# One core, two chained models: GpSimd's first load delayed, batch 0's softmaxes in parts, another order, and 40 pairs of unread matmuls

## The chip, the cores and the metric

The kernel runs on one core of one Trainium2 chip. The metric is device time in microseconds (us) of one execution; lower is better. Three runs of the kernel before gave 136.5 to 136.55, median 136.54. A separate execution was profiled; its own time was 136.75.

The core's engines work through queues of their own and wait for each other by semaphores: TensorE (PE; its weight loads are listed as PEld), VectorE (DVE), ScalarE (ACT), GpSimd (POOL) and SyncE (SP). SP, GpSimd and ScalarE can start transfers, which 16 DMA engines carry out.

## The reference

```
p_packed = softmax(scale * p @ k^T) @ v              # per batch and head: 32 rows attend to 576
x        = softmax(scale * q @ p_packed^T) @ p_packed   # 576 rows attend to the 32
x        = heads side by side: (8, 576, 512)
W        = scale * (x @ w_q) @ (x @ w_k)^T           # 576 x 576 per batch
out      = relu(W @ x) @ w_out                       # (8, 576, 512), float32
```

There are 8 batches, 8 heads, 576 positions, 64 numbers a head. All inputs and the output are float32; the kernel computes in bfloat16 behind its loads, with float32 sums.

## The kernel before, in words

One batch is one pass through about 70 small operations. Nothing is looped over them: the string SCHEDULE (lines 10 to 55) holds all operations of all 8 batches in one order, written `name@batch`, with the PSUM banks behind a colon (`s0` and `e0` use one buffer of three banks, psA, in turns) and the engine of an eviction as a last letter (v: VectorE, s: ScalarE). Lines 641 to 651 issue them in that order. Each engine takes its own from the string in order, so an instruction that waits holds up everything behind it on its engine.

The operations of a batch, in the order in which its data goes through them:

- LK, LV, LQ (L138): loads of K, V and Q with a cast to bfloat16, from GpSimd's queue, 576 KB each as landed, into six buffers per tensor. cw and wo load the weights in the same queue.
- kt, qt (L261): transposes of K and Q on TensorE, three parts each; ke, qe evict them from PSUM.
- s0 (L283): p times K. nm0 (L297): row maximum on VectorE. ex0, ex1 (L300): exponential on ScalarE, one per head half. rc1: reciprocal of the sums.
- xt, xe, pv, pp, pt, pte (L314 to L370): transposes of the exponentials, product with V, scaling, transposes of the packed rows; pq, pqe: their product with the mixer's weights.
- e0 (L388): Q times the packed rows. mx0, sb0, sm0, rr0 (L409 to L429): maximum, subtraction, sum and reciprocal on VectorE, x0 the exponential on ScalarE, ml0 to ml2 (L431) the division on GpSimd in three parts.
- at, ae, wk, wke, wkx, wq, wqe, g, ge, y, ye (L448 to L556): the mixer on the packed rows.
- m0, m1, m2 and r (L558 to L595): the mixed rows and their relu; o0 to o4 and oe (L597 to L611): the product with w_out and its eviction; st, sc (L613 to L632): stores from SP's queue, in blocks of 256 or 128 KB. m2, o4 and st2 exist once for two batches.

Batch 0 has a start of its own. SP loads p of batch 0 (p_f, L153), K of batch 0 in float32 in two halves (k_f, L156) and the whole of p (p_c, L161). cA and cB cast k_f (L216), kf and kfe transpose and evict it (L221, L231). tp and lp (L182, L188) put p of batch 0, transposed, into pT_bd, which holds p of all batches as the weights of s0; pc, tr and lq (L194 to L213) do that for the other seven. VectorE sets pT_bd and the two masks to zero and one (L164 to L172), while GpSimd makes the identity matrix (L177) behind its first load.

Of the kernel before, what the change touches and what calls it, by code (L numbers as in the profile page):

```python
# [9 lines left out]
SCHEDULE = """  # L10
    LK@1 cw2@0 LV@0 tp@0:0 LQ@0 lp@0v LK@2 cw0@0 cA0@0s cA1@0v LV@1 kf1@0:0 kf0@0:1 kfe1@0s
    LQ@1 kfe0@0v cB1@0s cB0@0s kf3@0:1 kfe3@0s kf2@0:0 kfe2@0s pc1@0v pc0@0v s0@0 LV@2 tr@0:01
    nm0@0 cw3@0 kt0@1:2 lq0@0s kt2@1:3 ke0@1v kt1@1:4 ke2@1v ex1@0 lq1@0v cw1@0 ex0@0 ke1@1v
    rc1@0 xt0@0:4 s0@1 xe0@0v xt1@0:1 nm0@1 xe1@0s qt0@0:4 LK@3 qt1@0:3 qt2@0:1 qe0@0v ex0@1
    pv@0:02 qe1@0v qe2@0s pp0@0 ex1@1 pp1@0 kt1@2:0 LK@4 rc1@1 pt@0:2 ke1@2v xt1@1:1 pte@0s
    kt0@2:3 wo0@0 xe1@1s xt0@1:4 ke0@2v kt2@2:2 e0@0 xe0@1v ke2@2v mx0@0 pv@1:24 LQ@2 sb0@0
    pp0@1 x0@0 s0@2 pp1@1 qt0@1:2 nm0@2 wo1@0 pt@1:4 qt2@1:3 pte@1s qt1@1:1 qe2@1s qe0@1v ex1@2
    sm0@0 ex0@2 LV@3 qe1@1v xt0@2:2 rc1@2 xt1@2:3 rr0@0 LV@5 pq@1:1 xe0@2v pq@0:4 xe1@2s e0@1
    LK@5 pqe@0s pqe@1s pv@2:32 mx0@1 ml2@0 ml0@0 pp1@2 kt2@3:1 ml1@0 pp0@2 at0@0:2 ke2@3s sb0@1
    kt0@3:4 pt@2:3 kt1@3:0 LQ@3 ae0@0s at1@0:1 pte@2s ke1@3v x0@1 pq@2:3 ae1@0v ke0@3v kt2@4:0  # L20
    LQ@4 pqe@2s wk@0:1 sm0@1 ke2@4s s0@3 wke@0s wq@0:0 LV@4 wkx@0 kt0@4:3 rr0@1 wqe@0s kt1@4:1
# [12 lines left out]
    ml1@3 kt0@7:3 pte@4s qe1@5v kt1@7:4 pq@4:2 ke0@7v qt0@6:1 ml2@3 pqe@4s qt2@6:0 ml0@3 ke1@7v
    at1@3:2 qe2@6s qe0@6v e0@4 ae1@3v g@2:1 mx0@4 at0@3:2 ge@2s qt1@6:0 ae0@3s y@2:1 pv@5:43
    ye@2v qe1@6v m0@2:12 sb0@4 wq@3:0 r00@2s r01@2s wk@3:1 pp0@5 wqe@3s s0@7 wkx@3 wke@3s pp1@5
    x0@4 o1@2:0 nm0@7 kt0@6:3 oe1@2s kt2@6:1 pt@5:4 ke0@6v ex0@7 kt1@6:0 sm0@4 o0@2:2 pte@5s
    ex1@7 qt0@7:4 pq@5:3 ke1@6v pqe@5s e0@5 qe0@7v ke2@6s oe0@2v g@3:3 m1@2:40 ge@3s mx0@5
    xt1@7:2 st0@2 r11@2s y@3:3 xt0@7:1 r10@2s qt2@7:0 xe0@7v xe1@7s o2@2:4 rr0@4 qe2@7s ye@3v
    ml0@4 o3@2:2 rc1@7 sb0@5 oe2@2s m2@3:4 ml1@4 oe3@2s at0@4:0 qt1@7:3 ae0@4v x0@5 s0@6 st1@2  # L40
    qe1@7v ml2@4 m0@3:02 nm0@6 pv@7:31 r2@3s r00@3s o4@3:4 r01@3s sm0@5 ex1@6 o1@3:2 oe4@3s
    pp0@7 pp1@7 at1@4:0 ex0@6 st2@3 o0@3:4 rr0@5 ae1@4v oe1@3s ml2@5 rc1@6 pt@7:1 ml1@5 oe0@3v
    wq@4:0 pte@7s wk@4:2 wqe@4s st0@3 ml0@5 pq@7:4 wkx@4 wke@4s xt0@6:1 pqe@7s at1@5:0 xe0@6v
    xt1@6:2 at0@5:4 ae1@5v xe1@6s e0@7 ae0@5s g@4:2 mx0@7 m1@3:01 ge@4s pv@6:43 r11@3s r10@3s
    sb0@7 y@4:1 wq@5:2 o3@3:0 wqe@5s pp0@6 x0@7 o2@3:2 pp1@6 ye@4v pt@6:3 oe3@3s sm0@7 wk@5:1
    pte@6s m1@4:04 oe2@3s pq@6:3 e0@6 wke@5s wkx@5 st1@3 r10@4s rr0@7 g@5:1 r11@4s mx0@6
    m0@4:02 ml0@7 ge@5s pqe@6s o3@4:4 r01@4s ml2@7 r00@4v ml1@7 y@5:2 o2@4:3 oe3@4s sb0@6
    o0@4:4 oe2@4s ye@5v x0@6 at1@7:3 st1@4 oe0@4v m2@5:2 o1@4:0 ae1@7v r2@5s sm0@6 at0@7:3
    oe1@4s o4@5:2 ae0@7s st0@4 m0@5:04 rr0@6 oe4@5s m1@5:31 r00@5v ml2@6 r01@5s wk@7:2 st2@5
    ml1@6 r11@5v r10@5s wq@7:4 wke@7s wkx@7 o1@5:1 ml0@6 wqe@7s at1@6:4 oe1@5s o0@5:2 ae1@6v  # L50
    at0@6:4 oe0@5v o3@5:1 ae0@6s st0@5 wk@6:4 oe3@5s g@7:2 wkx@6 wke@6s o2@5:1 ge@7s y@7:2
    wq@6:4 oe2@5s ye@7v g@6:3 wqe@6s st1@5 m1@7:12 ge@6s m0@7:40 r10@7s r11@7v y@6:3 r01@7s
    ye@6v o3@7:2 r00@7v o2@7:0 o1@7:4 oe2a@7v oe2b@7s m2@7:3 o0@7:1 oe1@7s sc2@7 r2@7s m0@6:40
    oe3@7s oe0@7v o4@7:3 sc1@7 r01@6s r00@6v m1@6:01 oe4a@7v oe4b@7s sc3@7 o0@6:4 r11@6s r10@6s
    o1@6:1 sc0@7 oe0@6v o3@6:0 oe1@6s st2@7 o2@6:1 oe3@6s st0@6 oe2@6s st1@6
"""

SLOTS = dict(
    k_sb=6, v_sb=6, q_sb=6, kT=3, qT=3, e1T=2, e1=2, pp=4, ppT=4, pqk=4, e2=2, a2=3, a2T=2,
    wk=2, wkx=3, wqT=2, g=2, y=3, reluT0=2, reluT1=2, reluX=2, o_sb0=2, o_sb1=2, ox=2,  # L60
    nmax=4, rsum=4, rrec=4, mx=2, rs=2, rr=2
# [4 lines left out]
def kernel(  # L66
# [12 lines left out]
    nc = tc.nc  # L79
# [12 lines left out]
    L = p.shape[2]  # L92
# [26 lines left out]
    def tile(name, shape, dtype, b, key=None):  # L119
        key = key or name  # L120
        if key not in S_[b]:
            S_[b][key] = sbp.tile(shape, dtype, tag=f"{name}{(b // 2 if name in PAIRED else b) % SLOTS[name]}", name=name)
        return S_[b][key]
# [36 lines left out]
    p_c = sbp.tile([P, 16, Dh], fp32, name="p_c")  # L160
    nc.sync.dma_start(p_c, p.rearrange("b h (lh lo) d -> (b h lh) lo d", lo=16))  # L161

    pT_bd = sbp.tile([P, B, 4, 2, L], bf16, name="pT_bd")
    nc.vector.memset(pT_bd, 0.0)  # L164
# [5 lines left out]
    nc.vector.memset(hmask, 0.0)  # L170
    for h2 in range(2):
        nc.vector.memset(hmask[64 * h2:64 * h2 + 64, :, h2], 1.0)  # L172

    ident_f = sbp.tile([P, P], fp32, name="ident_f")
    ident = sbp.tile([P, P], bf16, name="ident")

    def make_ident():  # L177
        make_identity(nc, ident_f)
        nc.vector.tensor_copy(ident, ident_f)
# [14 lines left out]
    for i in range(2):  # L194
        ops[f"pc{i}"] = lambda b, on, i=i: evict(on, p_b[:, 8 * i:8 * i + 8], p_c[:, 8 * i:8 * i + 8], scale=scale)
# [100 lines left out]
    @op  # L296
    def nm0(b):  # L297
        nc.vector.tensor_reduce(tile("nmax", [P, 2], fp32, b), S_[b]["s1"], axis=AX, op=MAX, negate=True)  # L298
# [109 lines left out]
    @op  # L408
    def mx0(b):  # L409
        nc.vector.tensor_reduce(tile("mx", [P, NU, 1], fp32, b), S_[b]["e"], axis=AX, op=MAX)  # L410

    @op
    def sb0(b):
        nc.vector.tensor_tensor(  # L414
            tile("e2", [P, NU, L], fp32, b), S_[b]["e"], S_[b]["mx"].to_broadcast((P, NU, L)), op=SUB
        )

    @op
    def x0(b):
# [262 lines left out]
```

## Time and profile before

| | |
|---|---|
| median of three runs | 136.54 us |
| the profiled execution: its time, its span | 136.75 us, 135.0 us |
| TensorE busy | 106.2 us (79%) |
| VectorE busy | 97.3 us (72%) |
| ScalarE busy | 88.2 us (65%) |
| GpSimd busy | 41.0 us (30%) |
| DMA written | 25.73 MB, 191 GB/s over the span |
| granted TensorE clock, mean | 0.97 |

The span runs from the first instruction to the last; the profiled execution's time has 1.75 us around it. A profile line such as "L288 PE MATMUL s<-kT,pT_bd" names the line of the kernel, the engine, the operation, and the tile written and the tiles read; evictions all carry the lines of one helper (L128 to L136) and are told apart by their tiles. In a timeline each row has the start, the busy time, the engine, the line, the operation and its count, and in brackets how long the engine had been idle and what released it. The rows of stages give a stretch, its length, the busy time of PE, PEld, DVE, ACT and POOL with their counts, the granted TensorE clock, the share of the DMA engines and GB/s.

### The profile page before, as it was taken

How to read it: one execution, taken by the hardware profiler on the slowest of the kernel's cores; microseconds unless marked ns; L12 is line 12 of the kernel's file. 1: busy time of each engine (PE TensorE's matmuls, PEld its weight loads, DVE VectorE, ACT ScalarE, POOL GpSimd, SP SyncE). 2: the span in 40 equal slices, each digit the busy share in tenths (PEclk: the TensorE clock that was granted, in tenths of full speed). 3: DMA queues.
4: the chain of work that ended last, by engine and by line, in shares of the span. 5: the costliest groups of instructions: out<-in, count | busy, mean ns of one | idle time of the engine just before them, and what ended most of it. 6: DMA issues, size and time to landing. Idle time of an engine off the chain costs nothing.

```text
span 135.0 us, 4579 instructions
## 1 busy us (share of the span) xinstructions
PE 106.2 (79%) x1993; PEld 77.1 (57%) x1993; DVE 97.3 (72%) x167; ACT 88.2 (65%) x175; POOL 41.0 (30%) x59
## 2 busy tenths in 40 slices
PE   1228668954988999999679985999999999999900
PEld 0216657843767568778458653675866656563400
DVE  5413767999899949999769985999699994445200
ACT  3244808247687996986765693999789895818610
POOL 6924124226938522154033000153302442000000
PEclk9999968999999999999999999999999999999985
DMA  3999999999999999999999998554702386655994
GB/s 50 306 311 208 207 205 207 208 199 212 202 211 198 207 209 246 313 210 247 278 206 252 236 208 150 113 130 124 195 5 61 112 215 162 174 144 114 205 222 164
DMA packets 18277, 25.73 MB, mean 191 GB/s; under 512 B 2512, under 2 KB 14800, under 8 KB 18256
## 3 DMA queue, kind: packets, MB, share of 16 engines
q0 software_dynamic: 13776, 14.22, 63.0%
q1 hardware_dynamic: 4480, 11.21, 29.9%
q8 instruction: 15, 0.25, 0.7%
q14 instruction: 6, 0.05, 0.1%
HBM read 30.21 MB, written 9.44 MB: 294 GB/s over the span
## 4 chain that ended last, share of the span: by engine, by line
PE 42%; DMA 31%; DVE 11%; ACT 6%; issue 3%; SPq 1%; DVEq 0%; ACTq 0%
DMA q_sb<-in_q_dram 22%; PE o_ps L602 13%; PE tp_h L266 6%; DMA k_f<-in_k_dram 5%; DMA out_dram<-o_sb 4%; PE tp_x L319 3%; PE s L288 3%; ACT o_sb L130 2%; PE pv L339 2%; DVE kT L136 2%; DVE e L414 2%; PE wq_ps L514 2%; PE e_ps L401 2%; DVE pp L347 2%; PE wk_ps L492 1%
## 5 line engine op out<-in xcount | busy, mean ns | idle before, releaser
L433 POOL TENSOR_TENSOR a<-e,rr 128x512 bf16<-128x512 f32 (+1 forms) x24 | 19.3, 832 | 41.7 <-DVE rr L429 37.7
L602 PE MATMUL o_ps<-w_out,reluT 128*64 128x512 bf16 x256 | 31.3, 380 | 0.3 <-DVE reluT L132 0.2
L602 PEld LDWEIGHTS <-reluT 128*64 128x64 bf16 x256 | 14.9, 110 | 10.6 <-issue 1.0
L130 ACT ACTIVATE o_sb<-o_ps 128x512 f32<-128x512 f32 (+1 forms) x24 | 14.0, 596 | 6.7 <-PE o_ps L602 3.8
L130 ACT ACTIVATE reluT<-m_ps 128x512 bf16<-128x512 f32 x25 | 13.8, 603 | 1.6 <-PE m_ps L564 1.6
L266 PE MATMUL tp_h<-ident,q_sb 128*64 128x128 bf16 x288 | 11.4, 229 | 2.5 <-DMA q_sb<-in_q_dram 2.5
L302 ACT ACTIVATE e1T<-s,nmax 128x576 bf16<-128x576 f32 x16 | 12.1, 755 | 0.8 <-DVE nmax L298 0.7
L266 PE MATMUL tp_h<-ident,k_sb 128*64 128x128 bf16 x252 | 10.4, 222 | 2.6 <-ACT wk L130 1.2
L266 PEld LDWEIGHTS <-q_sb 128*64 128x64 bf16 x288 | 9.9, 117 | 4.4 <-DMA q_sb<-in_q_dram 3.6
L298 DVE TENSOR_REDUCE nmax<-s 128x2 f32<-128x1152 f32 x8 | 10.8, 1347 | 1.9 <-PE s L288 1.9
L136 DVE COPY kT<-tp_h 128x768 bf16<-128x768 bf16 (+1 forms) x18 | 9.6, 548 | 3.3 <-PE tp_h L266 2.0
L421 ACT ACTIVATE e<-e 128x1152 f32<-128x1152 f32 x8 | 9.3, 1161 | 4.1 <-DVE e L414 4.1
L410 DVE TENSOR_REDUCE mx<-e_ps 128x36 f32<-128x1152 f32 x8 | 10.8, 1348 | 1.6 <-PE e_ps L401 1.5
L266 PEld LDWEIGHTS <-k_sb 128*64 128x64 bf16 x252 | 8.8, 110 | 4.0 <-DMA k_sb<-in_k_dram 2.2
L414 DVE TENSOR_TENSOR e<-e_ps,mx 128x1152 f32<-128x1152 f32 x8 | 10.8, 1350 | 0.2
L425 DVE TENSOR_REDUCE rs<-e 128x36 f32<-128x1152 f32 x8 | 10.8, 1344 | 0.2 <-ACT e L421 0.2
L319 PE MATMUL tp_x<-ident,e1T 128*64 128x128 bf16 x144 | 6.9, 232 | 4.4 <-DVE kT L136 2.3
L136 DVE COPY qT<-tp_h 128x768 bf16<-128x768 bf16 x16 | 8.4, 546 | 2.6 <-PE tp_h L266 2.6
L140 POOL DMA_DIRECT2D v_sb<-in_v_dram x8 | 6.0, 752 | 13.6 <-DMA v_sb<-in_v_dram 4.6
L136 DVE COPY o_sb<-o_ps 128x512 f32<-128x512 f32 (+1 forms) x9 | 6.0, 661 | 5.7 <-PE o_ps L602 3.8
L339 PE MATMUL pv<-v_sb,e 64*128 64x256 bf16 x144 | 9.2, 270 | 0.5 <-DVE kT L136 0.3
L288 PE MATMUL s<-kT,pT_bd 128*64 128x64 bf16 (+3 forms) x64 | 7.0, 328 | 1.9 <-DVE e L414 1.5
(86 smaller groups left out, 209.5 us busy)
## 6 DMA issues: line engine op xcount, KB each, us to landing
out_dram<-o_sb SPq DMA_DIRECT2D x28, 256.0 KB, 3.6
v_sb<-in_v_dram POOLq DMA_DIRECT2D x8, 576.0 KB, 18.0
q_sb<-in_q_dram POOLq DMA_DIRECT2D x8, 576.0 KB, 20.8
k_sb<-in_k_dram POOLq DMA_DIRECT2D x7, 576.0 KB, 16.0
k_f<-in_k_dram SPq DMA_DIRECT2D x2, 576.0 KB, 5.6
out_dram<-ox SPq DMA_DIRECT2D x8, 128.0 KB, 2.7
out_dram<-o_sb SPq DMA_DIRECT2D x8, 128.0 KB, 2.4
p_c<-in_p_dram SPq DMA_DIRECT2D x1, 512.0 KB, 8.8
```

What stands on the lines that cost most here:

```text
L130: nc.scalar.activation(dst, src, func, scale=scale)
L136: nc.vector.tensor_copy(dst, src)
L266: nc.tensor.transpose(tp[64 * g2:64 * g2 + 64, 2 * gp:2 * gp + 2, jj, :], S_[b][src][:, gp + 2 * g2, order[3 * t + jj]], ident,)
L288: nc.tensor.matmul(ps[64 * gp:64 * gp + 64, S * h2 + c0:S * h2 + c1], pT_bd[:, b, 2 * gp + h2].rearrange("d g l -> d (g l)"), S_[b]["kT"][ ...
L298: nc.vector.tensor_reduce(tile("nmax", [P, 2], fp32, b), S_[b]["s1"], axis=AX, op=MAX, negate=True)
L302: nc.scalar.activation(tile("e1T", [P, 2, S], bf16, b)[:, h2], S_[b]["s1"][:, h2], EXP, bias=S_[b]["nmax"][:, h2:h2 + 1], accum_out=rsum[: ...
L319: nc.tensor.transpose(tp[64 * h2:64 * h2 + 64, j - j0, :], S_[b]["e1T"][:, h2, 64 * j:64 * j + 64], ident,)
L339: nc.tensor.matmul(ps[h2], S_[b]["e1"][r, j, :], S_[b]["v_sb"][r, :, j, :].rearrange("s (g gp) d -> s gp g d", gp=2), start=(j == 0), stop ...
L410: nc.vector.tensor_reduce(tile("mx", [P, NU, 1], fp32, b), S_[b]["e"], axis=AX, op=MAX)
L414: nc.vector.tensor_tensor(tile("e2", [P, NU, L], fp32, b), S_[b]["e"], S_[b]["mx"].to_broadcast((P, NU, L)), op=SUB)
L433: nc.gpsimd.tensor_tensor(tile("a2", [P, NU, L], bf16, b)[:, r], S_[b]["e2"][:, r], S_[b]["rr"][:, r].to_broadcast((P, r.stop - r.start, L ...
L602: nc.tensor.matmul(ps[64 * g2:64 * g2 + 64], src[:, i, o + 64 * g2:o + 64 * g2 + 64], w_out[:, i, :], start=(i == 0), stop=(i == 3),)
```

## The change

What it does:

- GpSimd makes the identity matrix first, then sets pT_bd to zero and fills hmask (VectorE did both), and only then issues its first load, which is Q of batch 0 and no longer K of batch 1.
- p_c has no buffer of its own any more: it takes that of the second half of k_f, and is loaded when the last cast of k_f (cB1) is done.
- For batch 0, nm, mx, sb, x, sm and rr are split into two instructions each (A and B: head halves, or units 0 to 15 and 16 to 35).
- wm issues pairs of 512-column matmuls (identity times the first 512 columns of pT_bd) whose result nothing reads: 13, 3, 2, 5, 4, 2, 6, 1 and 4 pairs at nine places of the first part of the list.
- The whole list has another order, with other banks and other engines for some evictions. Stores of a block (sc) may be issued from ScalarE's queue; two of the last block's four are.

The diff, cut to its core:

```diff
+    LQ@0 tp@0:4 wm@13:0 LV@0 cw3@0 cw1@0 cA0@0s cA1@0v LK@1 lp@0v LK@2 kf0@0:4 wm@3:0 cw2@0
+    cB0@0s cB1@0v LQ@1 kfe0@0v kf3@0:3 kf1@0:2 kfe3@0s kf2@0:4 kfe1@0v wm@2:0 kfe2@0v pc1@0s
+    s0@0 pc0@0s wm@5:0 nmA@0 nmB@0 ex0@0 qt0@0:1 cw0@0 ex1@0 qt2@0:3 qe0@0v qt1@0:4 qe1@0s
+    rc1@0 xt1@0:0 qe2@0v xt0@0:2 xe1@0v tr@0:31 xe0@0s pv@0:40 lq0@0v lq1@0s LV@1 LK@3
+    wm@4:2 pp1@0 pp0@0 wo1@0 pt@0:2 wm@2:0 pte@0v e0@0 kt2@1:0 wo0@0 mxB@0 kt1@1:3 kt0@1:2
+    mxA@0 ke1@1s wm@6:1 sbB@0 ke2@1s sbA@0 xB@0 kt2@2:3 ke0@1v LQ@2 xA@0 kt1@2:1 smB@0 s0@1
+    ke1@2s LV@2 wm@1:0 rrB@0 ke2@2s nm0@1 kt0@2:1 ml2@0g wm@4:0 ke0@2s ml1@0g smA@0 ex1@1
+    qt0@1:1 LK@4 at1@0:4 rrA@0 ex0@1 qe0@1v pq@0:0 qt2@1:2 LV@3 qt1@1:1 qe2@1v pqe@0s
+    xt0@1:3 ml0@0g qe1@1s ae1@0v xt1@1:0 s0@2 rc1@1 xe0@1v xe1@1s at0@0:2 nm0@2 ae0@0s
+    pv@1:41 ex1@2 wk@0:0 pp1@1 pp0@1 wq@0:3 wke@0s wkx@0 ex0@2 pt@1:4 g@0:1 pte@1s ge@0v
...
+    oe1@6v st2@3 m1@7:32 o0@6:1 r10@7s r11@7v oe2@6s m0@7:03 o3@7:2 r00@7v r01@7s oe0@6v
+    o3@6:3 oe3@7s st0@6 m2@7:4 o1@7:1 r2@7s sc3@7p oe3@6s o4@7:0 oe1@7s o0@7:3 st1@6 sc1@7s
+    oe4a@7v oe4b@7v o2@7:4 oe0@7v st2@7 oe2a@7v oe2b@7s sc0@7p sc2@7s
...
-    p_c = sbp.tile([P, 16, Dh], fp32, name="p_c")
-    nc.sync.dma_start(p_c, p.rearrange("b h (lh lo) d -> (b h lh) lo d", lo=16))
+    def load_rest_of_p():
+        p_c = sbp.tile([P, 16, Dh], fp32, tag=f"q_sb{SLOTS['q_sb'] - 2}", name="p_c")
+        nc.sync.dma_start(p_c, p.rearrange("b h (lh lo) d -> (b h lh) lo d", lo=16))
+        return p_c
...
+    make_identity(nc, ident_f)
...
-    nc.vector.memset(pT_bd, 0.0)
+    nc.gpsimd.memset(pT_bd, 0.0)
...
+    for part, r in (("0", slice(0, 2)), ("A", slice(0, 1)), ("B", slice(1, 2))):
+        ops["nm" + part] = lambda b, r=r: nm(r, b)
...
+    UNITS = {"0": slice(0, NU), "A": slice(0, 16), "B": slice(16, NU)}
...
+    def wm(n, ks):
+        ps = bank(ks[0], [P, 512], fp32, "warm")
+        for _ in range(n):
+            for g2 in range(2):
+                nc.tensor.matmul(
+                    ps[64 * g2:64 * g2 + 64], ident[:, 64 * g2:64 * g2 + 64],
+                    pT_bd.rearrange("d b x g l -> d (b x g l)")[:, 0:512], start=True, stop=True,
+                )
...
+        if name == LAST_KCAST:
+            S_[0]["p_c"] = load_rest_of_p()
```

GpSimd's queue in the new order, from its first load: LQ@0 LV@0 cw3 cw1 LK@1 LK@2 cw2 LQ@1 cw0 LV@1 LK@3 wo1 wo0 LQ@2 LV@2, ml2@0 ml1@0, LK@4 LV@3, ml0@0, ml0@1 ml1@1 ml2@1, LQ@3 LK@5 LQ@4 LV@4 LK@6 LQ@6 LK@7 LQ@5, ml of batch 2, LV@5 LQ@7 LV@6, ml of batches 3 and 4, LV@7, and the other ml.

## The prediction

> **What bounds the kernel now.** I read the page's 40 slices first, then the stage table, the chain of work that ended last, and the timelines of the first 45 us and of the end.
>
> ```profile
> PE   1228668954988999999679985999999999999900
> DVE  5413767999899949999769985999699994445200
> PEclk9999968999999999999999999999999999999985
> DMA  3999999999999999999999998554702386655994
> ```
>
> Three stretches (3.4 us a slice): TensorE is thin until about 40 us, mostly full to 128 us, then idle. DMA is full to 84 us. The stage table gives sizes (the columns are PE, PEld, DVE, ACT, POOL busy):
>
> ```profile
> 0.00:10.00 10.00, 1.97 (x27) 1.44 (x27) 3.99 (x14) 3.62 (x5) 6.57 (x14) 1.00 0.84 222
> 10.00:20.00 10.00, 7.29 (x120) 5.96 (x118) 5.78 (x13) 4.29 (x11) 2.73 (x4) 0.90 1.25 207
> 20.00:30.00 10.00, 7.66 (x190) 6.78 (x187) 8.74 (x15) 4.82 (x9) 2.73 (x4) 0.93 1.26 205
> 30.00:40.00 10.00, 7.24 (x197) 6.03 (x192) 9.54 (x15) 7.61 (x17) 6.89 (x9) 1.00 1.22 207
> ...
> 128.20:135.00 6.80, 0.00 (x0) 0.00 (x0) 0.00 (x0) 0.58 (x1) 0.00 (x0) 0.68 0.71 192
> ```
>
> Of the span's 135.0 us TensorE is idle 28.8: 8.0, 2.7, 2.3 and 2.8 in these first stages, 6.2 between 40 and 128.2, and 6.8 behind its last matmul. The chain shows what ends the waits:
>
> ```profile
> 1.74 7.23 DMA k_f<-in_k_dram
> ...
> 53.67 29.52 DMA q_sb<-in_q_dram
> ...
> 83.23 0.53 PE tp_h L266 x12
> ...
> 128.18 0.60 ACT o_sb L130
> ```
>
> First the load of batch 0's K, at 83.2 us the last load of Q, and then TensorE to the end.
>
> **A yardstick.** One nominal price for each operation of the list, from uninterrupted pieces of that chain: kt, qt 0.35 us, s 0.61, xt 0.26, pv 0.99, pt 0.18, pq 0.11, e 0.63, at 0.22 and 0.34, wk and wq 0.46, g 0.30, y 0.11, m 0.33, m2 0.24, o 0.87. Both lists come to 95.1 us of TensorE without the unread pairs. "Lag" is clock time minus the nominal work ahead of a point. Before, it is 16.2 at e0@0 (9.0 us of work done at 25.2), 20.3 at e0@1 (13.2 at 33.5), 22.9 at m0@0 (22.7 at 45.6), 29.4 at qt0@7 (53.8 at 83.2), 30.3 at pv@6 (67.5 at 97.8) and 33.1 at the end (95.1 at 128.2). The last 27.6 us of work added 2.85: 0.103 per us, with TensorE full, so this is what the prices leave out.
>
> **Change 1: GpSimd starts later, K of batch 0 comes alone, p_c after it.** GpSimd now makes the identity and zeroes pT_bd and hmask ahead of its first load. No row shows a GpSimd memset of 2048 bf16. Its rows of 128x128 (225 ns) and 128x1 (102 ns) give 0.97 ns an element: 2.1 us, or 1.1 if it goes by words as DVE's row does (1024 words, 0.91 us). I take 2.1, since the change's instruction is over 2048 elements, so pT_bd is zero at 3.75 us and the first load is issued at 4.5 (before: 1.25). That row of DVE is 0.89 ns a word; "VectorE: DVE Perf Modes" (Zero memsets can be issued as uint32) of the Trainium skill says a memset costs a cycle per element whatever its type. It speaks against moving this one to an engine with no word form; by words the forecast would be 1.0 us lower. Transfers do not run dry, since k_f (1.18 MB at the 310 GB/s of slices 2 and 3) takes from about 2.7 to 6.5 us. It landed at 8.99 before, so 2.5 us seem to be won.
>
> **Change 2: 13 unread pairs come first.** They eat that. They need pT_bd, so they start at 3.75. At half clock a pair costs 0.427 us (s0@1 below: 1152 columns in 0.96 us of chain), at full clock 0.215 (o: four pairs in 0.87). All 13 slow are 5.5 us, eight slow and five fast 4.5; I take 5.25, to 9.0. lp writes pT_bd, which the pairs read, so it waits on DVE until 9.0, and cB1 is behind it: lp 0.7 to 9.7, cB1 0.55 to 10.25, kfe0 0.5, kfe1 and kfe2 0.5 each behind kf1 and kf2: s0@0 ends at 12.6 instead of 13.0.
>
> p_c is issued only behind cB1, at 10.3. Its one row:
>
> ```profile
> p_c<-in_p_dram SPq DMA_DIRECT2D x1, 512.0 KB, 8.8
> ```
>
> Before, it queued behind k_f and landed 2.1 us after it (8.99 to 11.07). A small load (p_f, 1.9 us) plus 2.1 is 4.0; the row itself is 8.8. I take 4.9, nearer the first because k_f no longer precedes it: landing at 15.2. Here is a new wait: pc1 and pc0 are now on ScalarE **ahead of ex0@0**. Queued behind them are both exponentials, and TensorE's xt@0 behind those. Two casts (0.6 each) and two exponentials (1.56 for both): 17.95, where before
>
> ```profile
> 15.06 0.74 ACT L302 ACTIVATE e1T<-s,nmax 128x576 bf16<-128x576 f32 x1
> 18.03 0.75 PE L319 MATMUL tp_x<-ident,e1T 128*64 128x128 bf16 x10 [2.33 <-DVE kT L136]
> 18.51 1.22 PE L288 MATMUL s<-kT,pT_bd 128*64 128x512 bf16 x8
> ```
>
> the exponentials ended at 16.6, but xt@0 still waited for DVE until 18.03. The early nmA and nmB are hidden behind p_c.
>
> **The clock.** s0@1 took 1.22 us at 18.5, the same eight matmuls 0.68 at 28.9. The granted clock was 0.52 in the window of 18.15 to 21.56, after TensorE's idle 15.0 to 18.0:
>
> ```profile
> 18.15:21.56 3.41, 3.41 (x60) 3.07 (x61) 2.28 (x4) 0.99 (x2) 0.51 (x2) 0.52 1.29 203
> ```
>
> The new list has nothing for TensorE between qt@0 (done about 14.4) and xt@0 (18.0), so I charge tr, pv and wm@4 behind it at the slow rate. "TensorE: Matmul & The Clock Gate" (Part 1) of the Trainium skill has the clock halved after an idle window of 3.4 us, which this row agrees with, and puts the ramp at under 1% of a typical kernel's span: by that, all 40 pairs could bring 1.35 us here at most. The other 27 pairs are wm@4 and wm@2 on batch 0's chain (1.7 us of the walk below) and the rest beside DVE's work.
>
> **Change 3: batch 0 in parts, other order.** Walk: xt@0 to 18.5, tr to 20.1, pv to 21.2, pp0 and pp1 on DVE to 22.1; wm@4 also waits for lq1@0 on ScalarE (21.3) and runs to 23.0, pt, pte 23.65, **e0@0 at 23.7** (25.2 before). Splits of the 1.35 us rows by units (20 and 16) plus 0.03 each: mxB, mxA, sbB, sbA end at 27.2 (before, sb0@0 at 28.9). Then ke0@1, smB, rrB, nm0@1, smA, rrA to 31.05, with the multiplications at 1.05 and 0.40 beside; the exponentials of batch 1 end at 31.7, its xe1 on ScalarE at 33.5, pv@1 at 34.5. So wk@0 starts at 34.5 with 12.9 us of work done: lag **21.6**. Before, at e0@1, it was 20.3: the new kernel is *behind* by 1.3 here, but batch 0 is four microseconds further (wk@0 was at 38.8), and its m and o, dense TensorE work that asks little of DVE, come next. e0@1 at 37.3 (lag 22.4), at0@1 at 46.5 (23.2 done, lag **23.3**, against 22.9 before).
>
> From there 71.9 us of work at 0.103 give 7.4. Loads: LQ@3 and seven more stand on GpSimd behind ml@1, whose rr0@1 comes at 43.6, so they are issued from 46.0. The loads issued earlier last until about 42.5 (from 2.5: k_f 3.8, p_c 1.7, weights 3.1, and eleven of 0.59 MB at 207 GB/s, 2.85 each), so DMA stands some 4 us. With 1.5 to the first bytes, 2.85 a load, and stores (3.8 per batch, 6.3 by then), K of batch 7 lands at 73.8 and is used at 48.5 + 25.9 = 74.4; Q of 5 lands at 76.7, needed at 76.4. These margins are smaller than their errors; I charge 1.0. Q of 7 lands at 82.4, and its first use has 37.2 us of work behind it (41.3 before): no wait at 58.0 + 26.9 = 84.9. So the lag ends at 23.3 + 7.4 + 1.0 = 31.7, TensorE at 126.8 (128.2 before).
>
> **Change 4: the end.** Before: o_sb out at 128.8, the last of four 256 KB stores issued at 130.2, 3.7 to landing, 1.1 to the end: 6.8. Now the last block is halved between DVE and ScalarE (0.42) and goes in 128 KB stores, two each from ScalarE's and SP's queue: second issue 1.0 after TensorE, 2.4 to landing, 1.1: **4.6**. ScalarE's other stores (sc1@7) cost it 1.2 us under o4 and o0 (1.8): hidden.
>
> **Sum.** Lag -1.4, end -2.2: span 131.4. The profiled execution took 136.75 for its 135.0, and the median of the runs is 0.2 less: 131.4 + 1.75 - 0.2 = **132.9**.
>
> **Rivals.**
> *A, slower: p_c late.* By the row of 8.8 us it lands at 19.1; ex0@0, then rr0@1, ml@1 and the eight loads slide 3.9 us, with next to no slack at K of batch 7: 136.8. It decides from about 19: at 20.1 it is 137.8. For: four 256 KB stores issued together at 49.0, under full loads, took 7.3 us, and eight loads are in flight. Against: the 2.1 us above. 0.18, with other shifts of 4 us on this chain.
> *B, the middle gains nothing.* If the lag grows from 23.2 us of work on as before (33.1 - 22.9 = 10.2), TensorE ends at 128.6 and only the end gains: 134.7. For: DVE was at 9.6 of 10 in 100 to 110 us, and ScalarE gets 2.6 us of evictions more. That the pairs do not hold the clock, so that the change does not do what it says, is cheap here: what comes ahead of p_c is hidden behind it, tr, pv and wm@4 are charged slow already, and 36 transposes of K at 46 instead of 28 ns are 0.6, to 133.5. Both 0.25.
> *C, a better start.* Memset by words (-1.0), p_c in 4.0 (-0.9), full clock early (-0.7): 130.3. 0.13.
> Forecast (131.5 to 134): 0.40. Within 0.2% of 136.54, about what a measurement of this kernel can tell from no change: 0.04. Faster: 0.40 + 0.25 + 0.13 = 0.78.
>
> Range: C's lower side, with no wait for loads, to 128.5; A at 19.7 to 137.4; about 0.1 is outside.
>
> **What the next profile should show.** First GpSimd load near 4.5 us; the 13 pairs from 3.75 to 9.0; pc1 starting at 15.2; xt@0 at 18.0; e0@0 at 23.7; wk@0 at 34.5; GpSimd's LQ@3 at 46; 4.6 us behind the last matmul. pc1 beyond 19 makes the forecast wrong, and so does wk@0 beyond 38.

## The result and the profile after

The changed kernel is **slower**: 141.62 us (median of 4 runs, 140.78 to 142.56) against 136.52 of the kernel before on the same chip, a ratio of 1.038 with a 95% interval of 1.032 to 1.044. The forecast was 132.9 us. Of each kernel, runs over 1.5% above its fastest count as slow: the ratios and their intervals leave them out, medians and ranges hold all runs. The profiled execution took 142.56 us, its span is 140.4 (before: 135.0). Its 40 slices, 3.5 us each:

```profile
PE   1979089999999999359989999994999999899500
PEclk9999955999999999999999999999689999999995
DMA  3999999999992199999999999993000585387874
```

TensorE's second to fourth slices are fuller (9, 7, 9; before 2, 2, 8), but the fifth (14 to 17.5 us) is empty, and behind it the clock is halved for two slices. DMA stands between 42 and 49 us. The holes of 56 to 63 and 95 to 98 us are new for TensorE. The stages (length, busy time of PE, PEld, DVE, ACT, POOL, clock, DMA share, GB/s):

```profile
10.00:20.00 10.00, 6.09 (x115) 4.66 (x113) 3.91 (x9) 4.16 (x9) 3.28 (x5) 0.86 1.26 228
20.00:30.00 10.00, 9.63 (x159) 6.49 (x155) 6.16 (x13) 4.29 (x10) 1.49 (x2) 0.79 1.24 206
...
40.00:50.00 10.00, 9.93 (x194) 7.23 (x194) 9.55 (x16) 8.95 (x17) 4.18 (x6) 1.00 0.48 84
50.00:60.00 10.00, 7.61 (x180) 6.04 (x178) 7.48 (x13) 6.40 (x14) 4.17 (x6) 1.00 1.07 204
...
131.84:140.40 8.56, 0.00 (x0) 0.00 (x0) 0.42 (x1) 0.38 (x1) 0.00 (x0) 0.79 0.66 187
```

TensorE is busier than before in the first 40 us (31.3 of 40 us against 24.2), partly with the unread pairs and partly at half clock; the time is lost from 50 us on and at the end. The chain that ended last, now (start, length, what):

```profile
3.45 4.78 PE warm L677 x26
...
9.46 6.39 DMA p_c<-in_p_dram
...
51.16 21.30 DMA k_sb<-in_k_dram
...
89.56 7.94 DMA out_dram<-o_sb
```

Before, K of batch 0, one load of Q and, near the end, two stores stood there. Now the waits are four others: the 13 unread pairs, the load of p_c behind them, a load of K issued at 51.16, and a **store**. The rows behind them, from the timeline:

```profile
15.88 1.15 ACT L134 ACTIVATE p_b<-p_c 128x512 bf16<-128x512 f32 x2 [4.83 <-DMA p_c<-in_p_dram]
17.80 0.32 PE L327 MATMUL tp_x<-ident,e1T 128*64 128x128 bf16 x1 [3.48 <-ACT e1T L310]
58.65 0.86 PE L270 MATMUL tp_h<-ident,q_sb 128*64 128x128 bf16 x24 [2.39 <-DMA q_sb<-in_q_dram]
62.52 0.53 PE L270 MATMUL tp_h<-ident,k_sb 128*64 128x128 bf16 x12 [1.69 <-DMA k_sb<-in_k_dram]
97.61 0.60 ACT L134 ACTIVATE o_sb<-o_ps 128x512 f32<-128x512 f32 x1 [2.78 <-DMA out_dram<-o_sb]
98.25 1.05 PE L631 MATMUL o_ps<-w_out,reluX 128*64 128x512 bf16 x8 [1.85 <-ACT o_sb L134]
```

The brackets read upwards in a chain: ScalarE stood 4.83 us for p_c, TensorE 3.48 for the exponentials behind ScalarE's two casts. Batch 0's division and the eight loads on GpSimd moved with that, and TensorE waited for Q and K (another 0.6 us at 72.5). At 97.6 an eviction waited for the store of its buffer, which landed at 97.5: st1@1 stands in the new list behind st0@2 and st1@2, so SP issued it at 88.4, though the list evicts its data much earlier.

### The profile page after: what moved, and what is told of

It reads as the page before. It is cut to its first block, busy times and chain, and to the rows that moved or that the text cites. A ratio compares the mean times of both kernels' runs of the same rounds, so it can differ in the third digit from the quotient of the medians.

```text
span 140.4 us, 4747 instructions
## 1 busy us (share of the span) xinstructions
PE 115.8 (82%) x2073; PEld 80.0 (57%) x2073; DVE 97.0 (69%) x167; ACT 90.4 (64%) x177; POOL 43.6 (31%) x63
## 4 chain that ended last, share of the span: by engine, by line
PE 41%; DMA 25%; DVE 11%; ACT 9%; POOL 3%; issue 3%; SPq 2%; POOLq 0%; DVEq 0%; ACTq 0%
DMA k_sb<-in_k_dram 15%; PE o_ps L631 14%; DMA out_dram<-o_sb 6%; PE warm L677 5%; DMA p_c<-in_p_dram 5%; PE tp_h L270 3%; ACT e1T L310 3%; PE pv L347 3%; PE m_ps L593 2%; DVE mx L424 2%; PE e_ps L409 2%; DVE e L427 2%; SPq L650 2%; PE tp_x L327 2%; PE wq_ps L543 2%
## 5 line engine op out<-in xcount | busy, mean ns | idle before, releaser
L134 ACT ACTIVATE kT<-tp_h 128x768 bf16<-128x768 bf16 (+1 forms) x12 | 9.2, 790 | 8.4 <-PE tp_h L270 5.6
L677 PE MATMUL warm<-pT_bd,ident 128*64 128x512 bf16 x80 | 12.6, 443 | 0.2 <-DVE mask L177 0.2
L424 DVE TENSOR_REDUCE mx<-e_ps 128x36 f32<-128x1152 f32 (+2 forms) x9 | 10.9, 1215 | 1.6 <-PE e_ps L409 1.4
L438 DVE TENSOR_REDUCE rs<-e 128x36 f32<-128x1152 f32 (+2 forms) x9 | 10.9, 1212 | 1.3 <-ACT e L434 1.2
L301 DVE TENSOR_REDUCE nmax<-s 128x2 f32<-128x1152 f32 (+1 forms) x9 | 10.8, 1207 | 0.9 <-PE s L292 0.8
L427 DVE TENSOR_TENSOR e<-e_ps,mx 128x1152 f32<-128x1152 f32 (+2 forms) x9 | 10.9, 1218 | 0.2
L347 PE MATMUL pv<-v_sb,e 64*128 64x256 bf16 x144 | 10.9, 301 | 0.0
L434 ACT ACTIVATE e<-e 128x1152 f32<-128x1152 f32 (+2 forms) x9 | 9.4, 1057 | 0.2 <-DVE e L427 0.2
L355 DVE SCALAR_TENSOR_TENSOR pp<-pv,rrec,mask 128x256 bf16<-128x256 f32 x16 | 7.1, 478 | 2.8 <-PE pv L347 2.6
L327 PEld LDWEIGHTS <-e1T 128*64 128x64 bf16 x144 | 5.8, 117 | 5.2 <-ACT e1T L310 4.2
```

Of the source, the lines that this page charges most:

```text
L134: nc.scalar.activation(dst, src, func, scale=scale)
L301: nc.vector.tensor_reduce(tile("nmax", [P, 2], fp32, b)[:, r], S_[b]["s1"][:, r], axis=AX, op=MAX, negate=True)
L327: nc.tensor.transpose(tp[64 * h2:64 * h2 + 64, j - j0, :], S_[b]["e1T"][:, h2, 64 * j:64 * j + 64], ident,)
L347: nc.tensor.matmul(ps[h2], S_[b]["e1"][r, j, :], S_[b]["v_sb"][r, :, j, :].rearrange("s (g gp) d -> s gp g d", gp=2), start=(j == 0), stop ...
L424: nc.vector.tensor_reduce(tile("mx", [P, NU, 1], fp32, b)[:, r], S_[b]["e"][:, r], axis=AX, op=MAX)
L427: nc.vector.tensor_tensor(tile("e2", [P, NU, L], fp32, b)[:, r], S_[b]["e"][:, r], S_[b]["mx"][:, r].to_broadcast((P, nu, L)), op=SUB,)
```

## The experiments

A table first; "before" is the kernel before, run beside it. The text goes by the medians, and says so where the ratios give another size.

| kernel | median us (range) | before | ratio, 95% |
|---|---|---|---|
| changed, again | 141.86 (140.5 to 143.3) | 136.32 | 1.035 [1.031, 1.040] |
| no pairs | 138.07 (137.7 to 139.4) | 136.28 | 1.016 [1.009, 1.022] |
| no first 13 pairs | 138.22 (136.3 to 140.2) | 136.39 | 1.006 [1.003, 1.009] |
| eight loads earlier | 138.44 (137.5 to 140.5) | 136.28 | 1.013 [1.007, 1.019] |
| store earlier | 140.27 (139.9 to 142.6) | 136.28 | 1.028 [1.024, 1.031] |
| casts of p_c later | 140.11 (138.8 to 142.0) | 136.28 | 1.019 [1.015, 1.022] |
| all last stores from SP | 142.20 (141.2 to 145.9) | 136.32 | 1.041 [1.037, 1.045] |
| all these, p_c late | 137.48 (135.9 to 140.6) | 136.32 | 0.999 [0.996, 1.002] |
| **p_c early alone** | 135.46 (133.9 to 136.7) | 136.32 | 0.991 [0.988, 0.994] |
| p_c early, no pairs | 134.72 (132.6 to 135.8) | 136.45 | 0.980 [0.975, 0.985] |
| p_c early, eight loads, store | 134.94 (133.5 to 136.6) | 136.45 | 0.985 [0.980, 0.989] |
| and a shorter end | 134.62 (134.1 to 135.6) | 136.45 | 0.987 [0.984, 0.991] |
| p_c early, store, end | 134.10 (133.7 to 135.5) | 136.32 | 0.985 [0.981, 0.989] |
| **p_c early, four loads, store, end** | 131.75 (130.9 to 132.6) | 136.32 | 0.966 [0.962, 0.970] |
| the same without pairs | 132.46 (131.6 to 133.9) | 136.32 | 0.970 [0.967, 0.973] |
| the same with pairs, p_c late | 135.68 (134.7 to 136.3) | 136.39 | 0.994 [0.991, 0.996] |
| kernel before, p_c late | 138.44 (137.8 to 140.8) | 136.45 | 1.015 [1.011, 1.019] |

**One term at a time, in the changed kernel.**

```diff
 no pairs:       -wm@13:0 -wm@3:0 -wm@2:0 ... (all nine)
 eight loads:    -ml2@1g pp0@2 at0@1:1 LQ@3 ... LK@5 ... LQ@4 ... LV@4 ... LK@6 ... LQ@6 ... LK@7 ... LQ@5
                 +ml0@0g LQ@3 LK@5 LQ@4 LV@4 LK@6 LQ@6 LK@7 LQ@5 ... ml0@1g
 store:          -st0@2 ... st1@2 ... st1@1          +oe2@1s st1@1 ... st0@2 ... st1@2
 casts:          -pc1@0s s0@0 pc0@0s ... ex0@0 ... ex1@0     +ex0@0 ... ex1@0 pc1@0s pc0@0s
```

Only the pairs, the loads, the store and the casts move; the other names show the place.

> The changed kernel without its 40 pairs of unread matmuls; all else as changed. Theory P (the pairs cost more than they bring): TensorE's 13 first pairs hold lp, cB1 and with it the load of p_c until 9.46 us, so without them p_c is issued about 7.4 and lands about 13.8 instead of 15.88; wk@0 comes about 2 us earlier than 36.4, and the time falls from 141.6 by 1 to 2 us. Rival Q (the pairs bring more than they cost): the clock stays at half until 20 us or later, s0@0 to e0@0 lengthen, and the time rises by 1 us or more. Rival L (what happens before 46 us does not matter, since the loads of batches 3 to 5 are issued behind ml@1): wk@0 moves, and the time with it, only as far as rr0@1 moves.

> The changed kernel with LQ@3 LK@5 LQ@4 LV@4 LK@6 LQ@6 LK@7 LQ@5 placed ahead of ml0@1 in GpSimd's queue instead of behind ml2@1. Theory L (the loads behind ml@1 leave DMA idle from 42 to 48 us, and TensorE later waits for the Q of batch 3, 2.4 us at 58.6, and for K, 1.7 at 62.5 and 0.6 at 72.5): DMA is full from 40 to 50 us, these three waits go, TensorE ends about 4 us earlier, 137 to 138.5 in all. Rival S (the late store of batch 1, which ScalarE waits for at 97.6, sets the end of the middle): the waits go, but the time given back there is lost again ahead of oe3@3, and the gain is under 2 us.

> The changed kernel with one item moved: st1@1, the store of batch 1's second half, comes right behind its last eviction oe2@1 in the list, not behind st0@2 and st1@2. Theory S (SP issues st1@1 20 us late, it lands at 97.5, and oe3@3, which writes the same buffer, blocks ScalarE and through it VectorE and TensorE; the clock then halves for 3.4 us): the wait of ScalarE for out_dram at 97.6 (2.8 us) and that of TensorE (1.85) go, the clock stays at 1.0 from 90 to 110 us, and the time falls by 2.5 to 3.5 us. Rival: another store or the load of V of batch 7 is in the way as well, and the wait only becomes shorter, under 1 us of gain.

> The changed kernel with pc1@0 and pc0@0 behind ex1@0 in the list, so that on ScalarE the exponentials of batch 0 no longer wait for p_c. Theory C (p_c ahead of ex0@0 costs the first stage 3 us and, by TensorE's idle time of 14.3 to 17.8, the clock): ex0@0 starts at about 13.0 instead of 16.9, xt@0 at about 14.7, TensorE idles less than a window and keeps the full clock, tr waits for p_c at 17, pv@0 ends at 18.5 to 19.5 instead of 23.4, and the time falls by 2 to 4 us. Rival L: rr0@1 comes earlier only in part, since batch 1 needs tr and lq behind p_c anyway, and the gain is under 1.5 us.

Without pairs 3.6 us less than the changed kernel's 141.62 (theory P had 1 to 2), with the loads earlier 3.2 less (as theory L had it), with the store earlier 1.4 and with the casts later 1.5 (both below what their theories had). The runs of the last two spread over 2.8 and 3.2 us; by the ratios they gain 1.0 to 1.4 and 2.3 to 2.7 us. Without pairs p_c was issued at 7.52 and e0@0 started at 22.86 (changed: 9.46 and 25.66). With the store earlier the waits behind it are gone, but the profile, which is of the longest of its runs, has TensorE wait 1.25 us for a load of Q at 84.1 and 1.07 for one of V at 95.0 instead. With the eight loads earlier TensorE was full from 50 to 80 us, but the store's hole remained:

```profile
50.00:60.00 10.00, 10.00 (x226) 8.09 (x221) 9.89 (x17) 8.52 (x18) 0.00 (x0) 1.00 1.17 258
...
70.00:80.00 10.00, 10.00 (x232) 7.69 (x228) 9.85 (x16) 9.93 (x19) 3.32 (x5) 1.00 1.10 189
...
90.00:100.00 10.00, 7.94 (x95) 5.00 (x92) 6.33 (x8) 5.64 (x12) 2.40 (x3) 0.83 0.16 57
```

With the casts behind the exponentials xt@0 started at 14.44, but TensorE then waited 2.82 us for p_b at tr: p_c itself came at 17.47 in that profile. So the order on ScalarE is not the whole cause; what it no longer holds waits for p_c a step later. How much the order costs by itself is open: that profile is of the longest run (142.01), and the two shortest ran at 138.8 and 139.0.

**The end, and everything at once.** sc1@7 and sc2@7, which are two stores each, went from ScalarE's queue to SP's, to take away a wait of SP that the end of the changed kernel shows (first row: 4.61 us for two issues, where others take 1.1 to 1.2):

```profile
130.52 4.61 SPq L650 DMA_DIRECT2D out_dram<-o_sb  x2
135.23 1.19 SPq L646 DMA_DIRECT2D out_dram<-ox  x2
```

> The changed kernel once more, on the chip of the three runs beside it. Both theories: 140.5 to 142.6 us, in two groups about 1.7 us apart, with p_c landing 6.4 to 8.2 us after its issue; if p_c is what spreads the runs, the longer ones have the later pc1.

> The changed kernel with sc1@7 and sc2@7 issued from SP's queue instead of ScalarE's, all else as changed. Theory T (the two queues share eight semaphores in turn, so the second store of st1@6 on SP waits 3.6 us for a store that ScalarE issued, and st2@7 and sc0@7 behind it go out 4 us late): the wait of SP goes, the end falls from 8.6 us behind the last matmul to about 7, and the time by 1 to 1.6 us. Rival: the DMA engines are the bound at the end (2.1 MB from 120 us on), so that SP's queue waits the same, and the time stays within 0.4 us.

> The changed kernel without the pairs, with the eight loads ahead of ml@1, st1@1 behind oe2@1, the casts of p_c behind ex1@0, and all stores from SP: the single edits so far, together. If the losses lie one behind another (pairs 3.1, loads 3.3, store 0.9, casts 2.0, tail 1.3 in the faster runs), they add up as far as they do not share the same wait: 131 to 133.5 us, faster than the kernel before. Rival: they hide each other (each of them only lets TensorE run into the next wait), and the sum is 135 or more.

The changed kernel came out again at 141.86. The theory on the end was right on the wait and wrong on the time, which stayed within the rival's 0.4 us. With all stores on SP the wait is gone, but SP has four more of them to issue, at about 0.6 us each, and the last one is hardly earlier (issued by 137.2 us, against 137.7):

```profile
131.69 1.67 SPq L655 DMA_DIRECT2D out_dram<-o_sb  x2
...
134.75 2.46 SPq L655 DMA_DIRECT2D out_dram<-o_sb  x4
```

This points to the number of stores that SP issues. What the wait is for can be read from the landings in the traces: the stores of SP and ScalarE signal their landing through eight semaphores, used in turn by both queues. In all ten profiles with this end, SP's waiting store went out 0.02 us behind the landing of ScalarE's first store, which has the same semaphore.

All the edits together, without pairs and with p_c still late, were level with the kernel before (137.48, spread over 4.8 us), as the rival had it. The profile, of the longest run, has a wait of 3.24 us for ml@1 in it, which comes up again below.

**p_c early.** One edit: p_c gets a buffer of its own again and is loaded right behind k_f; all else is as in the changed kernel.

```diff
+    p_c = sbp.tile([P, 16, Dh], fp32, name="p_c")
+    nc.sync.dma_start(p_c, p.rearrange("b h (lh lo) d -> (b h lh) lo d", lo=16))
+    S_[0]["p_c"] = p_c
...
-        if name == LAST_KCAST:
-            S_[0]["p_c"] = load_rest_of_p()
```

> The changed kernel with a buffer of its own for p_c and its load right behind k_f, as in the kernel before; pairs, order and all else as changed. Theory C (p_c, 6.4 to 8.2 us from issue to landing under the loads, holds the exponentials): p_c lands at 8 to 9.5 us, its casts are done before s0@0, ex0@0 starts at about 13, TensorE's idle time before xt@0 falls from 3.5 to under 1 us, and the time falls by 2.5 to 4 us. Rival P: the 13 pairs alone hold the start (lp at 8.3), so that the gain is under 1.5 us.

This alone brings **6.4 us** (141.86 to 135.46, measured side by side; theory C had 2.5 to 4) and turns the sign, if narrowly. In its timeline the hole is gone:

```profile
11.29 1.14 ACT L131 ACTIVATE p_b<-p_c 128x512 bf16<-128x512 f32 x2
14.14 0.74 ACT L306 ACTIVATE e1T<-s,nmax 128x576 bf16<-128x576 f32 x1 [1.71 <-DVE nmax L297]
15.02 0.24 PE L323 MATMUL tp_x<-ident,e1T 128*64 128x128 bf16 x1 [0.36 <-ACT e1T L306]
16.40 1.08 PE L202 MATMUL tp_r<-ident,p_b 128*64 128x128 bf16 x32
```

The casts no longer wait, ex0@0 waits for VectorE instead and starts 2.8 us earlier than in the changed kernel (14.14 against 16.93). TensorE stands 0.36 us instead of 3.48, the clock stays at 1.00, and tr, pv take 1.08 and 1.15 us instead of 2.02 and 2.10. e0@0 starts at 20.77 (25.66), wk@0 at 31.54 (36.43): 4.9 us. The other 1.5 fit the waits for Q and K, which shrank from 4.7 to 3.2 us.

**What is left, and how the gaps add up.** The pieces: the eight loads ahead of ml0@1; st1@1 right behind its cast; at the end two 256 KB stores for four of 128 KB (st0@7 for sc0@7 and sc1@7), and sc3@7 from ScalarE, so that 12 stores are left instead of 14, and SP issues 8 of them instead of 10.

```diff
 end:       -sc1@7s  -sc0@7p  +st0@7   -sc3@7p  +sc3@7s
```

> The changed kernel with three edits: p_c in its own buffer and loaded right behind k_f, the eight loads ahead of ml@1, st1@1 behind oe2@1; pairs kept. Theory: with p_c out of the way (135.5 alone), what is left in the middle are TensorE's waits for loads (2.1 + 1.1 us) and for the late store (1.6); both go, and the time falls to 131 to 133. Rival: TensorE already runs at 9.9 to 10 of 10 in most stages from 30 us on, and the waits only move to the end of the loads; 134 or more.

> The changed kernel with p_c early and without the 40 pairs. Theory Q (with p_c out of the way the pairs do what they are for: granted clock 1.0 from 10 to 30 us, against 0.86 and 0.79 with p_c late): without them the clock halves again for a window or two between 10 and 25 us and the time is 1 to 2 us above that of p_c early alone, 136.5 to 137.5. Rival P (the pairs are a loss in themselves, as when they were taken out alone, -3.8 us): lp and s0@0 come 2 us earlier and the time falls to 133 to 134.

> As e9_early_loads_store, and at the end st0@7 in two stores of 256 KB in place of sc0@7 and sc1@7 in four of 128, all four from SP, with sc3@7 from ScalarE's queue: SP has eight stores to issue behind the last evictions instead of ten, and none behind ScalarE's. Theory (the end is bound by SP's issues at 0.57 to 0.6 us each, not by the transfer): the 8.6 us behind the last matmul shrink to 6.5 to 7, and the time is 1.5 to 2 us below that of e9_early_loads_store. Rival (bytes are the bound): within 0.4 us of it.

Without pairs it was 134.72, between the numbers of theory Q and rival P. Next to nothing came of the loads: their waits were gone, but a new one stood in their place. GpSimd's queue in the kernel with eight loads earlier and p_c early, and TensorE's wait behind it:

```profile
33.91 0.74 POOL L141 DMA_DIRECT2D v_sb<-in_v_dram  x1 [0.78 <-DMA w_out<-in_moe_w_out_dram]
36.37 0.74 POOL L141 DMA_DIRECT2D k_sb<-in_k_dram  x1 [1.72 <-PE m_ps L589]
39.29 0.74 POOL L141 DMA_DIRECT2D q_sb<-in_q_dram  x1 [2.18 <-DMA v_sb<-in_v_dram]
...
44.67 0.74 POOL L141 DMA_DIRECT2D q_sb<-in_q_dram  x1 [1.82 <-DVE pp L351]
45.42 2.41 POOL L458 TENSOR_TENSOR a<-e,rr 128x512 bf16<-128x512 f32 x3
...
46.54 0.64 PE L479 MATMUL tp_a<-ident,a 128*64 128x128 bf16 x8 [2.81 <-POOL a L458]
```

From the fourth on the loads go out only every 2.5 to 2.9 us, and ml@1, which was ready at about 41 (it ran at 40.93 where the loads stood behind it), is held until 45.42; TensorE waits 2.8 us for it. Some releasers in these brackets are put down to whatever came last. The landings in the trace tell more: GpSimd's 29 loads use eight semaphores of their own in turn, and in all 19 profiles of this case each load was issued only once the load eight places before it had landed, 0.28 us behind that or later; in the rows above it was 0.28 to 0.53. The end did as expected, 7.0 us behind TensorE instead of 8.6, but the time fell by only 0.3, as the rival had it: that kernel's wait for ml@1 was 4.4 us instead of 2.8. So three more kernels: only the first **four** loads ahead of ml0@1, once with pairs and once without, and one with the loads where the change had put them.

```diff
-    ml0@0g LQ@3 LK@5 LQ@4 LV@4 LK@6 LQ@6 LK@7 LQ@5 ... ml0@1g ml1@1g ml2@1g
+    ml0@0g LQ@3 LK@5 LQ@4 LV@4 ... ml0@1g ml1@1g ml2@1g ... LK@6 LQ@6 LK@7 LQ@5
```

> The changed kernel with p_c loaded early in its own buffer, with store st1@1 right behind the cast it stores, with the end's 14 SP stores cut to 12 (one whole 256 KB store for two halves, one half issued by ScalarE), and with only four of the eight loads (LQ@3, LK@5, LQ@4, LV@4) moved ahead of ml0@1 on GpSimd; the other four stay behind ml2@1. Theory M: the 2.8 to 4.4 us that TensorE waited for ml@1 came from the later ones of the eight loads, each of which waits in GpSimd's queue for an earlier transfer to land; with four loads ahead of it ml@1 starts at about 42, the wait at the transposes of a is under 1 us, and the waits for Q3 and K stay under 1 us too, since DMA does not stand. Then 134.6 less about 3 us: 131 to 133. Rival N: already the first of the four must wait for a landing, so that the wait for ml@1 stays over 2 us and the time stays at 134 to 135.

> The same as the kernel with four loads, without the 40 pairs of unread matmuls. Theory: with p_c early the pairs neither bring nor cost much (134.7 without against 135.5 with them, their intervals overlap), so this comes within 0.8 us of the kernel with pairs, 131 to 133. Rival: the faster first stage without pairs (ex0@0 at 12.2 instead of 14.1) is kept to the end once the loads are no longer in the way: 1 us or more below the kernel with pairs.

> The changed kernel with p_c early, with store st1@1 right behind its cast and with 12 SP stores at the end instead of 14; the eight loads stay behind ml2@1 as in the changed kernel. Theory: the gaps add up: against 135.5 with p_c early alone, 1.6 us of the store's wait and 1.6 of the end go, 132.3; TensorE still waits some 3 us for loads of Q and K after 55 us. Rival: DVE, 9.6 of 10 busy between 100 and 110 us in the kernel before, is the bound of the second half, so that what a wait at 95 us gives is lost again behind it, and only the end's 1.6 us show: 133.9 or more.

Four loads: **131.75 us**, 4.6 below the kernel before and 10.1 below the changed one. ml@1 runs at 41.25, the loads behind it at 43.60 with no wait between them:

```profile
41.25 2.41 POOL L458 TENSOR_TENSOR a<-e,rr 128x512 bf16<-128x512 f32 x3 [6.43 <-DVE rr L437]
43.60 0.80 POOL L141 DMA_DIRECT2D k_sb<-in_k_dram  x1
```

Theory M held. One wait of 1.97 us, at the transposes of Q at 74.1, remains. With no load moved the time was 134.10, as the rival's number had it, but not by its cause: from 100 to 110 us TensorE was busy for 10.00 of 10 and VectorE for 9.18, and the waits for Q and K grew from 3.2 to 4.7 us and took back what the store's wait gave. Without pairs it was 132.46, 0.7 more (0.5 by the ratios, whose intervals overlap), where with p_c early and nothing else the kernel without pairs was 0.7 faster (1.5 by the ratios, whose intervals do not). So with p_c early the pairs bring little at best, and the sign is not settled.

**Two questions left.** How much of p_c's lateness is its own, and through which pairs do the pairs cost 3.6?

> The kernel before with one edit: p_c in the buffer of the second k_f half and loaded behind the last cast of k_f, as in the change; the casts stay on VectorE ahead of nm0@0. Theory C (this edit alone is the loss): the casts of k_f end at 10.25, p_c lands 6.4 to 8.2 us later at 16.7 to 18.5 instead of 11.07, nm0@0 starts at about 18 instead of 13.0, and the time rises by 3.5 to 5 us, to 140 to 141. Rival L (in the kernel before DMA is full to 84 us and the last Q sets the middle): a late start is made up while TensorE would wait for loads anyway, and the time rises by under 1.5 us.

> The changed kernel without its first 13 of 40 pairs of unread matmuls (the other 27 stay). Theory F: what the pairs cost in the changed kernel (141.9 with, 138.1 without all 40) they cost through these 13 alone, which hold lp on VectorE and behind it cB1 and with that p_c's load: p_c is issued at about 7.5 instead of 9.46, and the time is 137.5 to 139. Rival G: half of the cost is the other 27 on batch 0's chain (wm@4 and wm@2 between pv@0 and e0@0): 139.5 to 140.5.

> The kernel that ran at 131.75 (p_c early, four of the eight loads ahead of ml0@1, store st1@1 behind its cast, 12 SP stores at the end), with p_c late again, in k_f's buffer as in the changed kernel. Theory: p_c's late load costs the same here as there, about 6 us, since batch 0's chain delays everything behind it: 137 to 139. Rival: in the changed kernel part of the 6.4 us was the second half's waits, which a late first half ran into (load waits of 4.1 us against 3.3, the store's 1.85 against 1.6), so that here it costs 3 to 4.5 us only: 134.7 to 136.3.

The kernel before, with p_c in k_f's buffer and loaded behind the last cast (the casts on VectorE ahead of nm0@0), lost 2.0 us, between both numbers:

```profile
10.11 0.34 SPq L163 DMA_DIRECT2D p_c<-in_p_dram  x1
16.44 0.76 DVE L134 TENSOR_SCALAR p_b<-p_c 128x512 bf16<-128x512 f32 x2 [8.84 <-DMA p_c<-in_p_dram]
17.12 1.35 DVE L300 TENSOR_REDUCE nmax<-s 128x2 f32<-128x1152 f32 x1
```

nm0@0 is 4.1 us later there (13.0 before), and half of that is made up behind it: TensorE's waits for loads, 2.6 us in the kernel before, are gone. In the kernel of 131.75 late p_c costs 3.9 us, so the rival held: wk@0 is 6.4 us later (38.21 against 31.85; p_c took 8.1 us in that profile), but the wait of 1.97 is gone and TensorE is 9.6 to 10 of 10 busy from 50 to 100 us. Late p_c thus costs 2.0, 3.9 or 6.4 us; the traces put this down to whether what follows has waits to give up or runs into new ones. And in the changed kernel the pairs' cost is all in the first 13: without them alone 138.22, without all 40 138.07. They hold lp on VectorE, and behind it cB1 and the issue of p_c (7.64 without them, 9.46 with).

## Why the prediction was wrong, point by point

The steps that failed are four terms of the sum: the end (4.6 us, measured 8.6), the waits for loads (1.0, measured 4.7), a wait for a store (not in the sum, measured 1.85) and the clock (one window at half speed, measured two).

**First loads, 13 pairs, s0@0: right.** The memset of pT_bd took 1.80 us (2.1 forecast), GpSimd's first load went out at 3.76 (4.5), the pairs ran from 3.45 to 8.2 (3.75 to 9.0), p_c was issued at 9.46 (10.3), s0@0 ended at 12.2 (12.6).

**p_c: right in the wait, too low in the price, and by luck in time.** The forecast was 4.9 us to landing; it took 6.4:

```profile
p_c<-in_p_dram SPq DMA_DIRECT2D x1, 512.0 KB, 6.4
```

and 5.8 to 8.2 in the kernels of the experiments. As it was issued 0.8 us earlier than forecast, xt@0 still came on time, so this term is not where the 9 us were lost; that p_c must be late was taken as given and not priced against an early one. What the forecast had for the landing was a small load plus a difference between two landings; p_c met GpSimd's loads in full flight. "DMA: Bandwidth & Descriptors" of the Trainium skill (Queues, rings and completion order) says that each DMA engine takes turns between its queues. Half of the 244 GB/s that were moved between 9.46 and 15.88 us gives 4.3 us for 512 KB, and with the 2.0 us that the page has as the fixed part (Anatomy of one DMA, for GpSimd's loads) an estimate of 6.3; this trace agrees, 6.4. Four other profiles do not: at 234 and 235 GB/s the same working gives 6.5, and p_c took 8.1 or 8.2 us there, so this is not the whole of it.

**The clock: wrong.** xt@0 started on time (17.80; forecast 18.0), but e0@0 2.0 us late (25.66; 23.7). Half clock was charged to tr, pv and wm@4, but pv stood in the walk with 1.1 us, near its nominal 0.99, and xt at full clock too. The clock was halved for two windows and not for one:

```profile
17.28:24.10 6.82, 5.90 (x72) 4.33 (x74) 3.06 (x9) 3.78 (x10) 2.11 (x3) 0.50 1.28 203
```

xt's second part took 1.17 us, pv 2.04. TensorE was busy for only 2.49 us of the first window, since xt@0 came 0.5 us into it and waited again; the last section has what the other profiles say of this. wk@0 started at 36.43 instead of 34.5.

**The loads: right in the wait, 3.7 us too low.** DMA stood as forecast (share 0.48 in 40 to 50 us), but "these margins are smaller than their errors; I charge 1.0" was 4.7 in the trace.

**The store: not seen.** 1.85 us. The order of the stores was never compared, though it changed.

**The end: wrong in sign.** Forecast were 4.6 us behind TensorE, measured 8.6 (before: 6.8). The last block's own stores were counted, not the queue of SP that they join: it still has ten stores to issue from 127.6 us on, at about 0.6 us each, and one of the issues holds a wait of 3.5 (4.61 less the 1.1 of two issues). The last issue was forecast 1.0 us behind TensorE and ended 5.9 behind it. In the five kernels with 12 stores the end was 7.0 to 7.3 us.

The sum closes. Against the forecast span of 131.4 us, 140.4:

| term | forecast | measured | difference |
|---|---|---|---|
| start of wk@0 | 34.5 | 36.43 | +1.9 |
| waits for Q and K | 1.0 | 4.7 | +3.7 |
| wait for the store | 0 | 1.85 | +1.85 |
| other growth of the lag up to TensorE's end | 9.1 | 6.65 | -2.45 |
| behind TensorE | 4.6 | 8.6 | +4.0 |
| span | 131.4 | 140.4 | +9.0 |

The lags for the fourth row: 23.5 us at wk@0, 36.7 at TensorE's end, 13.2 in all, less 4.7 and 1.85. That row is luck: nothing in the forecast has the lag grow by 2.45 us less than before, and without it the span would have been 11.4 us off.

**The rivals.** A (p_c late) had the part of the change and the sign, but was to decide from a landing at 19. In the runs 15.9 was late enough: early p_c alone moves the time from one side of the kernel before to the other. What A lacked was the second window at half clock and the waits for loads that a late start runs into. Of B, neither the middle (TensorE ended 3.7 us later than before) nor the gain at the end came; its point that holding the clock with pairs is worth little held. That the pairs delay p_c through lp and cB1 was in the forecast's walk, but not priced as a loss. C did not happen.

**What the change is worth without its faults.** The kernel with p_c early, four loads ahead, the store behind its cast and 12 stores at the end keeps the order, the split softmaxes and the pairs, and ran at 131.75 us, 4.6 below the kernel before. That this is near the forecast is luck: the forecast had p_c late, and with p_c late this kernel ran at 135.68. So there is a gain in the change, and two groups of faults, each about as large, bury it: p_c early brings 6.4 us in the changed kernel and 3.9 with all else mended; loads, store and end bring 6.2 with p_c late (141.86 to 135.68) and 3.7 with it early.

Not settled: why p_c takes 5.8 us in one kernel and 8.2 in another, and why the kernels with the new order spread more from run to run than the kernel before. Late p_c spreads the old order too (3.0 us), but the kernels with p_c early spread as well.

## What to carry to other kernels

Before a load is put behind the release of another buffer, price its landing under the transfers that will be in flight, and count everything that is queued behind its first reader: here half a megabyte whose casts started 4.6 us later on one engine cost 6.4. On a queue that works in order, loads ahead of arithmetic help only as long as none of them has to wait for an older transfer, here the one eight places before it; four of eight was right, eight and none each cost 2 to 3 us more. At the end, count the stores that one queue has yet to issue, not only the last block's bytes.

## What the runs showed of the hardware

- A 512 KB load from SP, beside GpSimd's loads, took 5.8 to 8.8 us to land. Runs of one kernel with the new order spread over 1.5 to 4.8 us, with p_c early or late; those of the kernel before over 0.2 to 1.0.
- After TensorE's gap of 3.48 us the granted clock stayed at 0.50 for 6.82 us, two windows, though TensorE was busy for 5.9 of them. Ahead of TensorE's last matmul the 19 profiles have 23 such stretches: eight of two windows, fifteen of one (3.41 us). In the eight TensorE was busy for 39 to 73% of the first window, in the fifteen for 83 to 100%; in the window ahead of the stretch it was never busy for more than about half. "TensorE: Matmul & The Clock Gate" of the Trainium skill (Part 1) has full speed come back after one busy window of about 3.4 us; the traces agree, if a window counts as busy from somewhere between 73 and 83% on. Transposes count: in the two kernels without pairs and with p_c early whose clock was halved near 25 us, the first window was 98% transposes, and full speed came back behind it.
- With p_c early the 40 pairs hold the clock: it is 1.00 from 20 to 30 us with them and 0.83 without. It brings little: the medians differ by 0.7 us, once one way and once the other. With p_c late they do not: the changed kernel has two windows at half clock near 20 us, the same without pairs one.
- GpSimd's loads were issued 0.75 us apart at first and 2.5 to 2.9 us apart once eight were under way, and held the arithmetic behind them; SP's and ScalarE's stores share another eight semaphores. That it is the semaphores' turn and not another limit at eight was not tried by itself.
